# Four more query tiles turned by way of DRAM and VectorE in an adaLN block with linear attention

## The chip, the core and the metric

The kernel runs on one core of a Trainium2 chip. The metric is the device time of one execution in microseconds (us). Before the change three runs took 558.2, 560.55 and 560.79 us, a median of 560.55 us. A profile was taken of one more execution.

## What is computed

A block of x (2048 tokens of width 512, float32) with two halves. Each half normalises its input, scales and shifts it by vectors that come from a condition c, and adds a gated result to x.

```python
mod = (_silu(c) @ w_mod).reshape(1, 6, 1, -1)
sa, ca, ga, sb, cb, gb = (mod[:, i] for i in range(6))
h = _layernorm(x) * (1 + ca) + sa
x = x + ga * attention(h, wqkv, wo)
h = _layernorm(x) * (1 + cb) + sb
x = x + gb * (((h @ w_gate) * (h @ w_up)) @ w_down)      # 512 -> 1376 -> 512
...
# attention: 32 heads of 16
pq, pk = phi(q), phi(k)          # phi(t) = (t + 1 if t > 0 else exp(t)) + 1e-6
kv  = einsum("bhsd,bhse->bhde", pk, v)
z   = einsum("bhsd->bhd", pk)
num = einsum("bhqd,bhde->bhqe", pq, kv)
den = einsum("bhqd,bhd->bhq", pq, z)[..., None] + 1e-6
out = (num / den) @ wo
```

## The kernel before

**Tiles and stages.** The tokens lie in 16 tiles of 128 (numbered 0 to 15, so "tiles 5 to 8" counted from one are 4 to 7), four to a chunk. Every float32 product is made of three matmuls: both operands are split into a high part, made by ScalarE, and a low part, the difference, made by VectorE or GpSimd (`split`). The first stage makes k, sums up kv and z over all tiles and makes a part of q. The second makes W' = kv times wo with the gate ga in it (`w_out`), the denominators and, for each tile, y = x + (pq/den) W'. The third normalises y and runs the gated product over 1376 columns; three of its eleven column groups (`lone`) are computed early, while the attention of later chunks still runs, and the other eight in a block scheme with fewer products (`block`, `ffn`).

**The order of the work.** The program is written out by hand in the order in which each engine is to take its instructions; nothing is reordered. Each engine works through its own list and stops where an operand, or a buffer that is to be written, isn't ready. All transfers are issued by SP, one queue in that same order; a transfer whose source isn't there yet holds up those behind it. Eight semaphores go round among the transfers, so that each also waits for the one eight places before it. 94 buffers of 128 x 512 are handed out in turn, and so are eight banks of PSUM, four of them (`bank`) for passing results, four (`acc_bank`) for sums.

**One query tile, the first way (tiles 0 to 7).** `q_a` and `q_b` make phi(q). `den_a` multiplies it by z and sums over each head, `den_b` completes the denominators of a chunk and inverts them, `den_c` multiplies the tile by its inverse denominators. `turn_a` transposes the tile, which is 128 tokens by 512 columns, with four TensorE transposes into a bank (L672). `turn_h` (ScalarE) and `turn_l` (VectorE) split the result. `y_seed` copies x into a bank of sums (L746), and `y_a` adds twelve matmuls with W' (L755). `y_b` takes the sum back to SBUF with its statistics.

**The second way (tiles 8 to 15, `FLIPPED`).** `ready` is `den_c` and then `move_out`: the scaled tile is stored in DRAM. `move_in` fetches it back in four pieces, in which a 32-row block has become a column group. `turn_v` is one VectorE instruction that transposes 32 x 32 blocks (L722). Together they give the transposed tile with its columns in another order, and the matching W' has its rows in that order too (`wp4`): `wp_store` writes W' to DRAM, `wp_fetch` reads it back permuted. TensorE has no part in it.

**Around the change.** `y_step(i)` turns tile i + 1, makes y of tile i, splits and seeds tile i + 1 and takes back tile i - 1. `proj` makes q of a tile, `ln2_nx` normalises a chunk, `ln2_turn` transposes and modulates it, `gate_up` makes the two products of one of the `lone` groups and returns the rest (`g`), `split_gu`, `split_down` and `scale_down` prepare its weights. `by_fours` stores a column vector to DRAM, element by element, and fetches it back in groups of four for use much later (`flipped`). At the start of the third stage `right_sums` and `right_split` prepare the weights of the block scheme and `first[k].split` two of its left operands; `block` starts with its product of bank a, a second one in bank d, and a third one that adds to a copy of bank a.

Of the kernel before, what the change touches and what calls it, by code (L numbers as in the profile page):

```python
# [14 lines left out]
P = 128  # L15
# [9 lines left out]
def tile_adaln_block(  # L25
# [12 lines left out]
    nc = tc.nc  # L38
# [3 lines left out]
    KD = D // P  # L42
# [261 lines left out]
    def proj(i, w, of=bank):  # L304

        ch, j = divmod(i, NJ)
        ps = of()
        product(ps, [(cut(norm[ch].t[k], j * P, (j + 1) * P), w[k]) for k in range(KD)])
        return ps
# [48 lines left out]
    def q_b(i):  # L358
        phi_b(q_ps.pop(i), phq[i])
# [226 lines left out]
    def den_a(ch, *js, on=None):  # L586

        for j in js:
            den_p(ch, j, on=on)
            den_r(ch, j)  # L590
# [5 lines left out]
    def den_c(*tiles):  # L596

        for i in tiles:
            ch, j = divmod(i, NJ)
            p3 = phq[i].rearrange("p (h i) -> p h i", i=DH)  # L600
            nc.vector.scalar_tensor_tensor(p3, p3, EPS_PHI, dens[ch][:, j].unsqueeze(2).to_broadcast([P, NH, DH]),
                                           op0=ALU.add, op1=ALU.mult)
# [81 lines left out]
        turn_h(i)  # L684
        turn_l(i)

    FLIPPED = range(8, NT)
    SUMS = (0, 1, 2)
    wp4, moved = [], {}

# [49 lines left out]
    def y_seed(i, of=acc_bank):  # L740

        yps[i] = of()
        if of is bank:

            nc.tensor.matmul(yps[i], wp[0][0][:, :P], wp[0][0], start=True, stop=True)
        nc.scalar.activation(yps[i], xts[i // NJ][i % NJ], AF.Copy)  # L746

    def y_a(i):
# [17 lines left out]
    def y_step(i, *more, late=(), q=None, turn=True, seed=acc_bank):  # L766

        if q is not None:
            ps = proj(q, wq)
        if turn and i + 1 < NT and i + 1 not in pqs and i + 1 not in FLIPPED:  # L770
            turn_a(i + 1)
        y_a(i)
        if i + 1 in tps:
            turn_h(i + 1)
            turn_l(i + 1)
        if seed is acc_bank and i + 1 < NT:
            y_seed(i + 1, seed)
        if i - 1 in yps:
            y_b(i - 1)
        if q is not None:  # L780
            q_a(q, ps)
        if seed and i + 1 < NT and i + 1 not in yps:
            y_seed(i + 1, seed)
        for do in more:
            do()
        for do in late:
            do()
# [14 lines left out]
    def scale_down(f):  # L802
        d = raw_f[f][2]
        nc.vector.tensor_tensor(d, d, gb[:d.shape[0]], op=ALU.mult)  # L804

    def split_gu(f, low=None):
        n = fts[f][1]
        wf[f] = [split_raw(raw, (P, KD, n), low) for raw in raw_f[f][:2]]
# [62 lines left out]
    def ln2_nx(ch):  # L871
        norm2[ch].nmr_of()
        ln2_xhat(ch)

    def by_fours(col, name):

        t, v = consts.tile([P, KD], F32, name=name), tc.dram_tile([D], F32, name=name + "_row")
        nc.sync.dma_start(v.rearrange("(k p) -> p k", p=P), col)
        nc.sync.dma_start(t, v.rearrange("(p k) -> p k", k=KD))
        return t  # L880

    def stow(ch, *js):

# [29 lines left out]
    for f in lone:  # L913
        load_ffn(f)
    kept = [[tc.dram_tile([P, D], F32, name=f"kept_{ch}_{k}") for k in range(KD)] for ch in PLAIN]
    cb4, sb4 = by_fours(cb, "cb4"), by_fours(sb, "sb4")
    for ch in range(NCH):
        norm2[ch] = Norm(xts[ch])

# [290 lines left out]
    den_c(2)  # L1210
    q_a(11, ps)
    q_b(10)
    y_step(0, lambda: den_c(3), lambda: q_b(11))
    y_step(1)
    y_step(2, lambda: split_gu(f0, nc.gpsimd))
    y_step(3, lambda: scale_down(f0), wp_store, turn=False, seed=False)
    ps12 = proj(12, wq)
    y_b(3)
    norm2[0].rstd_of()
    den_a(1, 0, on=nc.vector)  # L1220
    q_a(12, ps12)
    ps13 = proj(13, wq)
    ln2_nx(0)
    q_b(12)
    den_a(1, 1, 2, on=nc.vector)
    q_a(13, ps13)
    ps14 = proj(14, wq, acc_bank)
    split_down(f0, nc.gpsimd)
    den_a(1, 3, on=nc.vector)
    den_b(1)  # L1230
    ln2_turn(0, 0, 1, cast=nc.vector)
    q_b(13)
    ps15 = proj(15, wq, acc_bank)
    ln2_turn(0, 2, 3, cast=nc.vector)
    q_a(14, ps14)
    den_c(4)
    q_b(14)
    q_a(15, ps15)
    split_gu(f1, nc.gpsimd)
    g = gate_up(0, f0)  # L1240
    q_b(15)
    den_c(5)
    scale_down(f1)
    g()
    turn(4)
    y_seed(4)
    split_gu(f2)
    g = gate_up(0, f1)
    den_a(2, 0, on=nc.vector)
    den_c(6)  # L1250
    split_down(f1, nc.gpsimd)
    g()
    y_step(4, lambda: scale_down(f2), lambda: den_a(2, 1, on=nc.vector))
    g = gate_up(0, f2)
    split_down(f2)
    den_c(7)
    den_a(2, 2, on=nc.vector)
    g()
    y_step(5, lambda: den_a(2, 3, on=nc.vector), wp_fetch)
    y_step(6, lambda: den_b(2), lambda: ready(8))  # L1260
    y_step(7, lambda: ready(9), lambda: move_in(8), turn=False, seed=False)
    y_b(7)
# [8 lines left out]
    ln2_turn(1, 2, 3)  # L1271
    y_step(9, lambda: turn_v(11))
    side.update(plain_side((0, 1)))
    first = [Left((0, 1), k).into(side) for k in range(KH)]
    for x in first:
        x.get("a21", "a22", "a11", "a12")
# [40 lines left out]
    first[1].sum("s1", "s3", "s2", "s4", on=nc.gpsimd)  # L1317
    y_seed(14, y_bank)
    turn_h(14)
    first[0].split("s1", "s2")  # L1320
    turn_l(14)
    y_b(13)
    y_seed(15, y_bank)
    right_sums(0, nc.vector)
    take()
    first[1].split("s1", "s2")
    turn_v(15)
    for n in range(4):
        banks.append(bank())
    banks[:] = [banks[n] for n in (2, 0, 1, 3)]  # L1330
    turn_bank[0] = acc_bank
    right_split(0)
    draw_load(0)
    stash, second_side, plan = {}, {}, {}
    work = ffn()
# [79 lines left out]
```

## Time and profile before

| | |
|---|---|
| runs | 558.2, 560.55, 560.79 us |
| profiled execution | 559.39 us |
| its span, first to last instruction | 557.7 us |
| granted TensorE clock, mean | 0.997 |
| TensorE matmul | 99% of the span |
| VectorE | 68% |
| ScalarE | 52% |
| GpSimd | 36% |

The page lists busy time by engine (PE is TensorE, DVE is VectorE, ACT is ScalarE, POOL is GpSimd, SPq the queue that issues transfers), groups of equal instructions, and a chain of waits: the work that ended last, followed back from the end, with start, length and name of each piece. The timeline has start, length, engine, line, operation, result and operands of each instruction; in square brackets stands how long the engine had been idle before it and what ended that. VectorE and ScalarE instructions overlap a little, so that the distance of two starts is less than the duration shown.

### The profile page before, as it was taken

How to read it: one execution, taken by the hardware profiler on the slowest of the kernel's cores; microseconds unless marked ns; L12 is line 12 of the kernel's file. 1: busy time of each engine (PE TensorE's matmuls, PEld its weight loads, DVE VectorE, ACT ScalarE, POOL GpSimd, SP SyncE). 2: the span in 40 equal slices, each digit the busy share in tenths (PEclk: the TensorE clock that was granted, in tenths of full speed). 3: DMA queues.
4: the chain of work that ended last, by engine and by line, in shares of the span. 5: the costliest groups of instructions: out<-in, count | busy, mean ns of one | idle time of the engine just before them, and what ended most of it. 6: DMA issues, size and time to landing. Idle time of an engine off the chain costs nothing.

```text
span 557.7 us, 7356 instructions
## 1 busy us (share of the span) xinstructions
PE 550.1 (99%) x2505; PEld 451.3 (81%) x2505; DVE 377.8 (68%) x605; ACT 291.4 (52%) x539; POOL 203.0 (36%) x203
## 2 busy tenths in 40 slices
PE   8999999999999999999899999999999999999997
PEld 6888888888888878878688888887888888888886
DVE  7896968977947886877877587886553544434435
ACT  3695856646477567566683545554444444444110
POOL 2000000101012300055698666566667446446200
PEclk9899999999999999999999999999999999999999
DMA  8900203220532605846435162591335222100004
GB/s 279 384 16 2 75 25 103 101 76 1 155 100 92 188 20 169 264 143 162 132 75 148 42 201 65 188 318 29 113 114 150 59 56 58 56 21 0 1 0 150
DMA packets 59141, 60.39 MB, mean 108 GB/s; under 512 B 8608, under 2 KB 37536, under 8 KB 59104
## 3 DMA queue, kind: packets, MB, share of 16 engines
q1 hardware_dynamic: 59104, 59.93, 34.3%
q8 instruction: 19, 0.31, 0.2%
q14 instruction: 18, 0.15, 0.1%
HBM read 43.65 MB, written 16.26 MB: 107 GB/s over the span
## 4 chain that ended last, share of the span: by engine, by line
PE 92%; DVE 3%; ACT 2%; DMA 1%; issue 1%; SPq 0%; DVEq 0%; ACTq 0%
PE bank L1026 32%; PE acc L1106 6%; PE acc L1107 6%; PE acc L1108 6%; PE acc L755 5%; PE bank L209 5%; PE bank L211 5%; PE bank L210 5%; PE acc L351 3%; PE acc L349 3%; PE acc L350 3%; PE bank L839 2%; PE bank L837 2%; PE bank L838 2%; PE bank L272 2%; DMA x<-in_A_x_dram 1%
## 5 line engine op out<-in xcount | busy, mean ns | idle before, releaser
L1026 PE MATMUL bank<-h,w 128*128 128x512 f32 (+1 forms) x798 | 185.4, 390 | 1.5 <-ACT bank L1031 1.5
L1026 PEld LDWEIGHTS bank<-h,w 128*128 128x128 f32 (+1 forms) x798 | 148.1, 186 | 35.8 <-ACT bank L1031 2.6
L1031 ACT ACTIVATE bank<-bank 128x512 f32<-128x512 f32 (+1 forms) x38 | 22.1, 583 | 137.1 <-PE bank L1026 137.0
L824 DVE TENSOR_TENSOR x<-acc,x 128x512 f32<-128x512 f32 (+1 forms) x73 | 48.4, 681 | 47.4 <-PE acc L1108 47.3
L1012 POOL TENSOR_TENSOR w<-raw,w 128x256 fp32r<-128x256 f32 (+3 forms) x38 | 41.3, 1086 | 95.2 <-ACT w L1005 95.2
L1107 PE MATMUL acc<-w,kh 128*128 128x512 f32 (+2 forms) x154 | 59.6, 387 | 0.0
L1106 PE MATMUL acc<-w,kh 128*128 128x512 f32 (+2 forms) x154 | 59.6, 387 | 0.0
L1108 PE MATMUL acc<-w,kl 128*128 128x512 f32 (+2 forms) x154 | 59.5, 386 | 0.0
L197 POOL TENSOR_TENSOR w<-raw,w 128x512 fp32r<-128x512 f32 (+1 forms) x25 | 36.0, 1442 | 55.3 <-ACT w L196 28.5
L250 POOL TENSOR_TENSOR rstd<-ve,half 128x4 f32<-128x4 f32 (+1 forms) x10 | 10.8, 1080 | 120.7 <-DVE ve L249 68.0
L1012 POOL TENSOR_TENSOR w<-t,w 128x512 fp32r<-128x512 f32 (+1 forms) x38 | 49.3, 1320 | 0.0
L197 DVE TENSOR_TENSOR kl<-u,kh 128x512 fp32r<-128x512 f32 (+1 forms) x38 | 26.4, 733 | 30.2 <-ACT kh L196 30.2
L209 PE MATMUL bank<-w,h 128*128 128x512 f32 x104 | 40.8, 392 | 0.0
L211 PE MATMUL bank<-w,h 128*128 128x512 f32 x104 | 40.5, 390 | 0.0
L210 PE MATMUL bank<-w,h 128*128 128x512 f32 x104 | 40.5, 389 | 0.0
L755 PE MATMUL acc<-w,xh 128*128 128x512 f32 x120 | 37.7, 395 | 0.0
L1106 PEld LDWEIGHTS acc<-w,kh 128*128 128x128 f32 (+1 forms) x154 | 28.9, 188 | 6.0
L1108 PEld LDWEIGHTS acc<-w,kl 128*128 128x128 f32 (+1 forms) x154 | 28.9, 188 | 5.9
L1107 PEld LDWEIGHTS acc<-w,kh 128*128 128x128 f32 (+1 forms) x154 | 28.9, 188 | 5.9
L1085 DVE TENSOR_TENSOR u<-bank,u 128x512 f32<-128x512 f32 (+1 forms) x19 | 13.1, 687 | 28.9 <-PE bank L1026 22.9
L259 ACT ACTIVATE n<-x,nmr,rstd 128x512 f32<-128x512 f32 x30 | 22.9, 804 | 12.2 <-DVE nmr L254 12.2
L196 ACT ACTIVATE w<-raw 128x512 fp32r<-128x512 f32 (+2 forms) x44 | 26.3, 619 | 1.9 <-DVE raw L804 1.0
(206 smaller groups left out, 1125.1 us busy)
## 6 DMA issues: line engine op xcount, KB each, us to landing
raw<-in_w_mod_dram SPq DMA_DIRECT2D x24, 256.0 KB, 3.8
raw<-in_B_w_down_dram SPq DMA_DIRECT2D x20, 256.0 KB, 3.2
raw<-in_B_w_gate_dram SPq DMA_DIRECT2D x36, 128.0 KB, 3.7
raw<-in_B_w_up_dram SPq DMA_DIRECT2D x36, 128.0 KB, 3.6
x<-in_A_x_dram SPq DMA_DIRECT2D x16, 256.0 KB, 5.7
out_dram<-x SPq DMA_DIRECT2D x15, 256.0 KB, 2.6
raw<-in_A_wqkv_dram SPq DMA_DIRECT2D x12, 256.0 KB, 5.4
wp<-w SPq DMA_DIRECT2D x8, 256.0 KB, 3.3
```

What stands on the lines that cost most here:

```text
L196: nc.scalar.activation(h, src, AF.Copy)
L197: (low or nc.vector).tensor_tensor(l, src, f32(h), op=ALU.subtract)
L209: nc.tensor.matmul(ps, ah, bh, start=i == 0, stop=False)
L210: nc.tensor.matmul(ps, ah, bl, start=False, stop=False)
L211: nc.tensor.matmul(ps, al, bh, start=False, stop=i == n - 1)
L755: nc.tensor.matmul(yps[i], x, y, start=False, stop=k == KD - 1 and x is al, skip_group_check=True)
L824: nc.vector.tensor_tensor(xt[:, a:b], dn[j][:, a:b], xt[:, a:b], op=ALU.add)
L1012: sub = lambda out, x, y: (on or nc.gpsimd).tensor_tensor(out, x, f32(y), op=ALU.subtract)
L1026: mm = lambda x, y, **kw: nc.tensor.matmul(ps, x[:, k], y, skip_group_check=True, **kw)
L1106: nc.tensor.matmul(ps, hh[:, a:b], dh[:n, c:d], start=i == 0, stop=False)
L1107: nc.tensor.matmul(ps, hh[:, a:b], dl[:n, c:d], start=False, stop=False)
L1108: nc.tensor.matmul(ps, hl[:, a:b], dh[:n, c:d], start=False, stop=i == len(hs) - 1)
```

## The change

Tiles 4 to 7 go the second way as well. For this `FLIPPED` starts at 4, `wp_store` stands behind `y_step(0)` and `wp_fetch` behind `y_step(2)`, the denominators of the second chunk are made between the steps of the first, and the calls of `ready`, `move_in`, `turn_v` and, for tile 4, `turn_h` and `turn_l` take the places of `den_c` and `turn`. `by_fours` is cut in two: the store stays, the fetch, which waits for it, is issued behind `y_step(9)`. `y_seed` no longer opens a passing bank with a matmul. At the start of the third stage the order of `turn_v(15)`, `turn_h(15)`, `right_sums`, the splits and `take` is another, and the four banks of the block scheme are no longer permuted.

```diff
-    FLIPPED = range(8, NT)
+    FLIPPED = range(4, NT)
...
     def y_seed(i, of=acc_bank):
 
         yps[i] = of()
-        if of is bank:
-
-            nc.tensor.matmul(yps[i], wp[0][0][:, :P], wp[0][0], start=True, stop=True)
         nc.scalar.activation(yps[i], xts[i // NJ][i % NJ], AF.Copy)
...
         nc.sync.dma_start(v.rearrange("(k p) -> p k", p=P), col)
-        nc.sync.dma_start(t, v.rearrange("(p k) -> p k", k=KD))
-        return t
+
+        def back():
+            nc.sync.dma_start(t, v.rearrange("(p k) -> p k", k=KD))
+            return t
+        return back
...
-    cb4, sb4 = by_fours(cb, "cb4"), by_fours(sb, "sb4")
+    back = by_fours(cb, "cb4"), by_fours(sb, "sb4")
...
-    y_step(0, lambda: den_c(3), lambda: q_b(11))
-    y_step(1)
-    y_step(2, lambda: split_gu(f0, nc.gpsimd))
-    y_step(3, lambda: scale_down(f0), wp_store, turn=False, seed=False)
+    y_step(0, lambda: den_c(3), lambda: q_b(11), wp_store)
+    y_step(1, lambda: den_a(1, 0, on=nc.vector))
+    y_step(2, lambda: split_gu(f0, nc.gpsimd), wp_fetch)
+    den_a(1, 1, on=nc.vector)
+    y_step(3, lambda: scale_down(f0), turn=False, seed=False)
+    den_a(1, 2, 3, on=nc.vector)
+    den_b(1)
     ps12 = proj(12, wq)
     y_b(3)
     norm2[0].rstd_of()
-    den_a(1, 0, on=nc.vector)
+    ready(4)
     q_a(12, ps12)
     ps13 = proj(13, wq)
+    ready(5)
     ln2_nx(0)
     q_b(12)
-    den_a(1, 1, 2, on=nc.vector)
+    ready(6)
+    move_in(4)
     q_a(13, ps13)
     ps14 = proj(14, wq, acc_bank)
     split_down(f0, nc.gpsimd)
-    den_a(1, 3, on=nc.vector)
-    den_b(1)
+    ready(7)
+    move_in(5)
     ln2_turn(0, 0, 1, cast=nc.vector)
     q_b(13)
     ps15 = proj(15, wq, acc_bank)
     ln2_turn(0, 2, 3, cast=nc.vector)
+    move_in(6, 7)
     q_a(14, ps14)
-    den_c(4)
+    turn_v(4)
     q_b(14)
     q_a(15, ps15)
     split_gu(f1, nc.gpsimd)
     g = gate_up(0, f0)
     q_b(15)
-    den_c(5)
+    turn_v(5)
     scale_down(f1)
     g()
-    turn(4)
+    turn_h(4)
+    turn_l(4)
     y_seed(4)
     split_gu(f2)
     g = gate_up(0, f1)
+    turn_v(6)
     den_a(2, 0, on=nc.vector)
-    den_c(6)
     split_down(f1, nc.gpsimd)
     g()
     y_step(4, lambda: scale_down(f2), lambda: den_a(2, 1, on=nc.vector))
     g = gate_up(0, f2)
+    turn_v(7)
     split_down(f2)
-    den_c(7)
     den_a(2, 2, on=nc.vector)
     g()
-    y_step(5, lambda: den_a(2, 3, on=nc.vector), wp_fetch)
+    y_step(5, lambda: den_a(2, 3, on=nc.vector))
...
     side.update(plain_side((0, 1)))
+    cb4, sb4 = (x() for x in back)
     first = [Left((0, 1), k).into(side) for k in range(KH)]
...
     turn_h(14)
-    first[0].split("s1", "s2")
+    turn_v(15)
+    right_sums(0, nc.vector)
     turn_l(14)
+    turn_h(15)
     y_b(13)
     y_seed(15, y_bank)
-    right_sums(0, nc.vector)
+    first[0].split("s1", "s2")
+    right_split(0)
+    first[1].split("s1", "s2")
     take()
-    first[1].split("s1", "s2")
-    turn_v(15)
+    turn_l(15)
     for n in range(4):
         banks.append(bank())
-    banks[:] = [banks[n] for n in (2, 0, 1, 3)]
     turn_bank[0] = acc_bank
-    right_split(0)
     draw_load(0)
```

## The prediction

> **What bounds the kernel now.** I read the page's first part, then TensorE's waits.
>
> ```profile
> span 557.7 us, 7356 instructions
> PE 550.1 (99%) x2505; PEld 451.3 (81%) x2505; DVE 377.8 (68%) x605; ACT 291.4 (52%) x539; POOL 203.0 (36%) x203
> ...
> PE bank L1026 <- ACT bank L1031: 1.5, 1, 1.5
> ```
>
> TensorE is busy 550.1 of 557.7 us. Past the start it waits once, at the first products of the last stage (1.5). So a gain can only be TensorE work that goes, or that 1.5; and every new wait of TensorE is lost whole. The chain of waits shows what the transposes cost, and what holds up the 1.5:
>
> ```profile
> 185.65 0.44 PE bank L672 x4
> ...
> 192.22 2.75 PE acc L755 x12
> ...
> 203.71 0.44 PE bank L672 x4
> 204.14 5.49 PE acc L755 x24
> ...
> 238.15 0.24 PE bank L839
> ...
> 263.79 2.29 DVE h L197 x2
> 266.08 1.02 DVE f L722
> ...
> 267.66 0.59 ACT bank L1031
> ```
>
> Four transposes take 0.44 us, and one matmul in a full stream 0.23 to 0.24. The last rows are the wait: VectorE turns tile 15 (`turn_v(15)`, L722) only at 266.08, behind two low parts that took 2.29. ScalarE's `turn_h(15)` waits for that, and the copy of bank a into bank b (L1031), on which TensorE's third product hangs, stands behind `turn_h(15)`.
>
> **The change part by part.** *Removed on TensorE*: 16 transposes (tiles 4 to 7; the first and the last four stand above), 4 x 0.44 = 1.76 us, and the matmul that opened tile 8's bank, 0.23. All lie in TensorE's unbroken stream: together 1.99.
>
> *The wait at 268*. `turn_v(15)` now stands right behind `turn_v(14)` (256.10, in the fence on VectorE's prices below) and takes 1.02 as at 266.08, so it ends near 258.2 and `turn_h(15)` soon after; the copy's place on ScalarE is then free. Gain 1.51, as that wait has it. What is late next: ScalarE now makes the four high parts of `right_split(0)` ahead of `first[1].split`.
>
> ```profile
> 263.89 0.62 ACT L1008 ACTIVATE w<-raw 128x512 fp32r<-128x512 f32 x1
> ...
> 263.59 3.19 PE L1026 MATMUL bank<-h,w 128*128 128x512 f32 x12
> 268.29 3.02 PE L1026 MATMUL bank<-h,w 128*128 128x512 f32 x12 [1.51 <-ACT bank L1031]
> ...
> 263.73 3.50 POOL L1012 TENSOR_TENSOR w<-t,w 128x512 fp32r<-128x512 f32 x2
> ```
>
> ScalarE is through with those at 264.4, so the first high part of `first[1]` is there at 265.0 and its low part, in the stretch where two of them took 2.29 beside GpSimd, at about 266.1. The second product wants it at its fifth matmul, 263.59 + 10 x 0.227 = 265.9. I charge 0.3: nothing if the low part takes 0.69 alone, 1.4 if it waits out GpSimd's pair (to 267.2).
>
> *Added on VectorE*: four turns for tiles 4 to 7, in place of four scalings (`den_c`, L601) that go forward into 169 to 174.
>
> ```profile
> 183.22 0.68 DVE L601 SCALAR_TENSOR_TENSOR h<-h,den 128x512 f32<-128x512 f32 x1
> 183.82 1.28 DVE L317 SCALAR_TENSOR_TENSOR h<-acc,h 128x512 f32<-128x512 f32 x2
> 185.02 0.94 DVE L601 SCALAR_TENSOR_TENSOR h<-h,den 128x512 f32<-128x512 f32 x1
> 185.89 1.78 DVE L804 TENSOR_TENSOR raw<-raw,row 128x512 f32<-128x512 f32 x1
> ...
> 189.57 0.68 DVE L680 TENSOR_TENSOR xl<-bank,xh 128x512 fp32r<-128x512 f32 x1
> ...
> 192.65 1.06 DVE L601 SCALAR_TENSOR_TENSOR h<-h,den 128x512 f32<-128x512 f32 x1
> 193.64 0.68 DVE L846 TENSOR_TENSOR phi<-bank,phi 128x512 f32<-128x512 f32 x1
> ...
> 198.74 0.68 DVE L601 SCALAR_TENSOR_TENSOR h<-h,den 128x512 f32<-128x512 f32 x1
> 199.34 0.68 DVE L578 TENSOR_TENSOR f<-h,zb 128x512 f32<-128x512 f32 x1
> ...
> 200.66 0.68 DVE L846 TENSOR_TENSOR phi<-bank,phi 96x512 f32<-96x512 f32 x1
> ...
> 256.10 1.10 DVE L722 STREAM_TRANSPOSE f<-u 128x512 f32<-128x512 f32 x1
> ```
>
> By the starts the scalings took 0.60, 0.87, 0.99 and 0.60 = 3.06; four turns of 1.02 take 4.08. VectorE so has 1.02 more here, less a head start: the second half of `ln2_turn(0)` hangs on ScalarE (179.76, below), and with no denominators queued VectorE is done with it at 182.6 instead of 183.22. It reaches the product of `gate_up(0, f2)` (L846, 200.66) 1.02 - 0.6 = 0.4 late, while TensorE comes 1.76 early. Who waits for it: that product releases ScalarE's split, then `turn_h(6)`, then tile 6's seed, one behind the other.
>
> ```profile
> 179.76 1.45 ACT L284 ACTIVATE f<-bank,col,col 128x512 f32<-128x512 f32 x2 [2.17 <-PE bank L272]
> ...
> 201.37 0.63 ACT L196 ACTIVATE kh<-phi 96x512 fp32r<-96x512 f32 x1 [0.93 <-DVE phi L846]
> ...
> 202.39 0.59 ACT L746 ACTIVATE acc<-x 128x512 f32<-128x512 f32 x1
> ```
>
> The seed (L746) ends at 202.98, and 203.4 after the change. `y_a(6)` stands in the chain at 204.14, where each matmul is entered at the end of the one before, about 0.23 after its own start; less that and less 1.76 it would start at 202.15. TensorE waits 203.4 - 202.15 = 1.25; I charge 1.3. Bounds: 0 if VectorE is not late (the seed then goes with TensorE), 1.25 + 0.6 + 0.27 + 0.39 = 2.5 if the head start of 0.6 goes and two turns are stretched as the scalings at 185.02 and 192.65 were. Tile 4 has room: its low part (189.57) came at 190.25, and `y_a(4)`, 192.22 in the chain, goes 0.88 forward, to 191.3.
>
> [...]
>
> *Moved forward on VectorE*: four `den_a` of 1.32 each (L578 and its sum, 199.34 to 200.66) and `den_b`.
>
> ```profile
> 169.07 0.17 DVE L247 TENSOR_SCALAR ve<-sums 128x4 f32<-128x4 f32 x1 [5.02 <-ACT acc L238]
> ...
> 171.43 2.92 ACT L259 ACTIVATE n<-x,nmr,rstd 128x512 f32<-128x512 f32 x4
> ...
> 175.67 0.87 PE bank L272 x8
> ```
>
> VectorE idled 5.02 ahead of `rstd_of` (L247), and some more between the tiles' low parts. Ten operations at 0.66 are 6.6, of which about 6 find a place there, so L247 comes some 0.5 late and the four normalisations (L259, done at 174.35) at most as much; TensorE transposes them at 175.67. The cover is 1.3, and I charge nothing; if GpSimd's splits drag the products out by 2, 1.2 would be lost.
>
> *Moved and added on SP's queue*: four stores and sixteen fetches of the tiles; the stores of wo' (`wp_store`) and the refetch (`wp_fetch`) early; the two fetches of `by_fours` late.
>
> ```profile
> 162.58 4.88 SPq L695 DMA_DIRECT2D wp<-w  x8
> 176.95 4.61 SPq L286 DMA_DIRECT2D kept<-f  x4
> ...
> w<-wp SPq DMA_DIRECT2D x8, 256.0 KB, 5.9
> moved<-h SPq DMA_DIRECT2D x8, 256.0 KB, 2.1
> u<-moved SPq DMA_DIRECT2D x32, 64.0 KB, 2.0
> cb_row<-col SPq DMA_DIRECT2D x1, 2.0 KB, 8.8
> ...
> 145.03 0.42 SPq L878 DMA_DIRECT2D cb_row<-col  x1
> ```
>
> Before, the stores of wo' began at 162.58, behind the two fetches that wait for scattered stores of 8.8 us. Now they go out as wo' is split, the last two after the scatters, 145.03 + 8.8 = 153.8 and a little; eight issues of 0.61 and a landing of 5.9 bring the refetch in before 170, against a first use (`y_a(4)`) near 191. Tile 4 is scaled at 170, stored by 172.4, issued back behind tile 6's store by 174.7 (0.43 each) and landed at 176.7; VectorE takes it at 182.6: 5.9 of cover. Tiles 6 and 7 stand behind the four stores of `kept` (to 181.6), land at 185.6 and 187.7, and are taken at 191.3 and 198. I charge nothing. The late `by_fours` fetches put 0.7 ahead of loads that are used many microseconds later: nothing, and 0.7 if that were wrong.
>
> *Sum*: -1.76 - 0.23 - 1.51 + 1.3 + 0.3 = -1.9. The profiled execution took 559.39 us, 557.7 of it the span; that gives 557.5. It lies 1.16 under the median of 560.55 (runs 558.2 to 560.79), so the forecast is 0.34% under its own execution and 0.54% under the median.
>
> **The rivals.** *VectorE keeps up.* TensorE gains all: 559.39 - 3.5 = 555.9. For it: 1.1 of the 1.78 at 185.89 is waiting beside GpSimd, and may shrink. Against: the products at 193.64 and 200.66 come without idle time of VectorE before them, so added work there shows.
>
> *VectorE sets the pace in both stretches.* If the head start goes and the charges reach their upper ends (2.5 + 1.4), the gain is undone: 559.39 - 3.5 + 3.9 = 559.8. For it: the stretch below, where VectorE (the third pair) is busy 9.86 of 10. Against: the 5 us of idle ahead of 169 take up most of what is moved.
>
> ```profile
> 178.00:188.00 10.00, 10.00 (x51) 8.02 (x50) 9.86 (x16) 5.34 (x9) 3.00 (x2) 1.00 0.74 222
> ```
>
> [...]
>
> *The turn waits for its transfer (slower).* `turn_v(4)` stands at VectorE's head at 182.6; behind it are `q_b(14)`, `q_b(15)`, the product of `gate_up(0, f0)` and all later low parts, and TensorE waits for those. From a landing at 183.7 (tile 4's low part has 191.3 - 190.25 = 1.05 of room) each microsecond is TensorE's. If store and fetch each took the 8.8 of the scatter, tile 4 would land at 170 + 8.8 + 1.8 + 8.8 = 189.4, 6.8 late, and tile 6's seed as much later than charged; with the 1.3 + 0.3 that is 559.39 - 3.5 + 6.8 + 1.6 = 564.3. Against: the landings of this very kind are 2.1 and 2.0.
>
> **How the numbers follow.** What this kernel's measurement can tell from no change is about 0.5%, 2.8 us. Chances: forecast 0.55, VectorE keeping up 0.20, pace 0.10, transfer 0.15. Against the median of 560.55 the line for faster is 557.75; the forecast lies just below it, and of its 0.55 I give 0.32 to faster and 0.23 to the same. With 0.19 of 0.20 from the first rival, faster is 0.51; the same is 0.23 + 0.01 + 0.10 = 0.34; slower 0.15. The predicted time is 557.5. The range goes from 555.4 (all 3.5 gained, and a run 0.5 lower) to 560.4 (nothing gained, and a run 0.5 higher), which leaves the transfer's case out.
>
> **What would show it.** The wait of TensorE on L1031 at 268 is gone, and `turn_v(15)` ends before 260. The chain has a stretch of VectorE and ScalarE ahead of `y_a(6)`, with TensorE idle 1.3 there. The second product of the last stage waits a few tenths on a low part (L197). No turn of tiles 4 to 7 waits for a transfer. It would be wrong if TensorE waited on `turn_v(4)`'s chain before 192, if the transposes at 175.67 came late, or if the stall at 268 were still there under another name.

## The result, and the profile after

Seven runs of the changed kernel took 561.56 to 565.03 us, a median of 563.06; beside them the kernel before took 558.55 (seven runs, 558.2 to 560.79). The ratio is 1.0069 with a 95% interval of 1.0044 to 1.0095: the change makes the kernel 0.7% slower. The profiled execution took 563.06 us, 561.4 of it the span, where the one of before had 557.7. The page and TensorE's waits:

```profile
span 561.4 us, 7362 instructions
PE 551.5 (98%) x2488; PEld 450.9 (80%) x2488; DVE 384.3 (68%) x609; ACT 291.6 (52%) x539; POOL 202.4 (36%) x203
...
PEclk9999999999999999999799999999999999999999
...
PE bank L1026 <- DVE h L197: 3.4, 2, 2.4
PE acc L148 <- DVE w L143: 2.0, 1, 2.0
PE acc L752 <- ACT acc L743: 0.9, 1, 0.9
```

17 matmul records fewer, and still 1.4 us more busy time. The wait on L1031 is gone; in its place stand 0.9 ahead of tile 6 and two waits, 3.4 together, at L1026 on VectorE's low parts (L197). The clock row has a 7 in one slice, in the same place. Four points of TensorE's timeline, in each kernel the first y matmul of the second stage, the first of tile 14, the first of tile 15, and one group of the block scheme behind it. Before:

```profile
155.41 0.70 PE L755 MATMUL acc<-w,xh 128*128 128x512 f32 x2
...
260.86 0.39 PE L755 MATMUL acc<-w,xh 128*128 128x512 f32 x1
...
271.15 0.61 PE L755 MATMUL acc<-w,xh 128*128 128x512 f32 x2
...
302.53 0.84 PE L1026 MATMUL bank<-h,w 128*128 128x512 f32 x3
```

After:

```profile
154.83 0.70 PE L752 MATMUL acc<-w,xh 128*128 128x512 f32 x2
...
259.42 0.62 PE L752 MATMUL acc<-w,xh 128*128 128x512 f32 x2
...
268.28 0.62 PE L752 MATMUL acc<-w,xh 128*128 128x512 f32 x2
...
306.25 0.62 PE L1026 MATMUL bank<-h,w 128*128 128x512 f32 x2
```

Two stretches by engine, before and then after; the column behind POOL is the granted clock:

```profile
10.00:20.00 10.00, 9.77 (x51) 8.01 (x52) 8.70 (x18) 8.31 (x14) 0.00 (x0) 0.83 1.05 391
274.50:281.20 6.70, 6.70 (x31) 5.53 (x31) 4.86 (x8) 2.50 (x6) 6.59 (x6) 1.00 0.25 65
```

```profile
10.00:20.00 10.00, 10.00 (x61) 8.38 (x60) 8.53 (x18) 8.11 (x14) 0.00 (x0) 1.00 1.05 390
274.50:281.20 6.70, 5.45 (x13) 4.30 (x14) 4.55 (x7) 1.11 (x2) 1.92 (x2) 0.50 0.17 42
```

The first pair of points differs by 0.58, which is no work of the change: from 10 to 20 us this execution of before had a clock of 0.83, that of after 1.00. (Of the fourteen kernels profiled for this text, the four whose clock falls early have the first point at 155.24 to 155.51, with the tiles or without, and the ten others at 154.21 to 154.94. Three of the four have 0.83 there, before, the new opening alone and the later rounding; the fourth, the rounding put back with the denominators behind, has an 8 in the clock row's slice from 14 to 28 us.) From the first point to the second the change gains 0.86 (105.45 to 104.59), to the third 1.43 more (10.29 to 8.86: the wait at 268 is gone), and to the fourth it loses 6.59 (31.38 to 37.97). Together -0.58 - 0.86 - 1.43 + 6.59 = +3.72, the difference of the spans. So one stretch of some ten microseconds takes back the gain three times over.

Here is that stretch, first before (VectorE's four low parts of s3 and s4, ScalarE's first rounding of the second k side, and GpSimd's low parts of it):

```profile
271.19 2.49 DVE L197 TENSOR_TENSOR h<-s,h 128x512 fp32r<-128x512 f32 x4
...
272.68 0.42 ACT L1005 ACTIVATE w<-raw 128x256 fp32r<-128x256 f32 x1
...
273.18 1.70 POOL L1012 TENSOR_TENSOR w<-raw,w 128x256 fp32r<-128x256 f32 x1 [4.73 <-ACT w L1005]
274.85 2.54 POOL L1012 TENSOR_TENSOR w<-t,w 128x512 fp32r<-128x512 f32 x2
277.34 1.29 POOL L1012 TENSOR_TENSOR w<-raw,w 128x512 fp32r<-128x512 f32 x1
```

and after, with TensorE's two waits:

```profile
270.56 5.73 DVE L197 TENSOR_TENSOR h<-s,h 128x512 fp32r<-128x512 f32 x4
...
268.97 0.41 ACT L1005 ACTIVATE w<-raw 128x256 fp32r<-128x256 f32 x1
...
269.45 0.90 POOL L1012 TENSOR_TENSOR w<-raw,w 128x256 fp32r<-128x256 f32 x1 [2.27 <-DMA u<-stowed]
270.32 3.15 POOL L1012 TENSOR_TENSOR w<-t,w 128x512 fp32r<-128x512 f32 x2
273.44 1.70 POOL L1012 TENSOR_TENSOR w<-raw,w 128x512 fp32r<-128x512 f32 x1
...
272.39 0.97 PE L1026 MATMUL bank<-h,w 128*128 128x512 f32 x3 [0.99 <-DVE h L197]
275.75 8.57 PE L1026 MATMUL bank<-h,w 128*128 128x512 f32 x25 [2.39 <-DVE h L197]
```

ScalarE came to L1005 3.7 us sooner (272.68 to 268.97) and VectorE to its low parts only 0.6 (271.19 to 270.56). Before, VectorE was 2.0 ahead of GpSimd and done when the latter had hardly begun; now GpSimd is 1.1 ahead, and the four low parts take 5.73 in place of 2.49. It isn't that both run slower for some reason: alone VectorE needs 2.49 and GpSimd 2.54 + 1.29 for the last three, 6.32 in sum, and together they took 270.32 to 276.29, 5.97. They ran nearly one after the other. The products s3 x t3 wait for it: from the matmul at 271.01 to 275.75 TensorE does four in 4.74, where four take 0.91, a loss of 3.83. Its clock is at 0.50 from 274.5 to 281.2 (the last row of the windows above), so that from 275.75 on it loses half of 5.45, 2.73. 3.83 + 2.73 = 6.56 of the 6.59.

This collision is the first theory for the experiments (Theory A below); that the waits bring the clock down is its second half.

### The profile page after: what moved, and what is told of

The parts are those of the page before. It is cut to its first block, busy times and chain, and to the rows that moved or that the text cites. A ratio compares the mean times of both kernels' runs of the same rounds, so it can differ in the third digit from the quotient of the medians.

```text
span 561.4 us, 7362 instructions
## 1 busy us (share of the span) xinstructions
PE 551.5 (98%) x2488; PEld 450.9 (80%) x2488; DVE 384.3 (68%) x609; ACT 291.6 (52%) x539; POOL 202.4 (36%) x203
## 4 chain that ended last, share of the span: by engine, by line
PE 88%; DVE 6%; ACT 3%; issue 1%; DMA 1%; SPq 0%; DVEq 0%; ACTq 0%
PE bank L1026 32%; PE acc L1107 6%; PE acc L1106 6%; PE acc L1108 6%; PE bank L209 5%; PE bank L210 5%; PE bank L211 5%; PE acc L752 4%; PE acc L351 3%; PE acc L350 3%; PE acc L349 3%; PE acc L148 2%; PE bank L272 2%; DVE h L197 1%; DVE f L722 1%
## 5 line engine op out<-in xcount | busy, mean ns | idle before, releaser
L1026 PE MATMUL bank<-h,w 128*128 128x512 f32 (+1 forms) x798 | 188.6, 394 | 3.4 <-DVE h L197 3.4
L1026 PEld LDWEIGHTS bank<-h,w 128*128 128x128 f32 (+1 forms) x798 | 149.8, 189 | 39.3 <-DVE h L197 4.7
L1031 ACT ACTIVATE bank<-bank 128x512 f32<-128x512 f32 (+1 forms) x38 | 22.1, 583 | 138.8 <-PE bank L1026 138.8
L821 DVE TENSOR_TENSOR x<-acc,x 128x512 f32<-128x512 f32 (+1 forms) x73 | 48.4, 680 | 47.4 <-PE acc L1108 47.4
L1012 POOL TENSOR_TENSOR w<-raw,w 128x256 fp32r<-128x256 f32 (+3 forms) x38 | 41.6, 1095 | 93.7 <-ACT w L1005 91.4
L197 POOL TENSOR_TENSOR w<-raw,w 128x512 fp32r<-128x512 f32 (+1 forms) x25 | 34.9, 1401 | 56.3 <-ACT w L196 56.3
L1012 POOL TENSOR_TENSOR w<-t,w 128x512 fp32r<-128x512 f32 (+1 forms) x38 | 49.4, 1319 | 0.0
L197 DVE TENSOR_TENSOR kl<-u,kh 128x512 fp32r<-128x512 f32 (+1 forms) x38 | 26.8, 745 | 31.6 <-ACT kh L196 31.6
L1085 DVE TENSOR_TENSOR u<-bank,u 128x512 f32<-128x512 f32 (+1 forms) x19 | 13.1, 689 | 27.9 <-PE bank L1026 21.7
```

The lines of the kernel that those rows point to most:

```text
L197: (low or nc.vector).tensor_tensor(l, src, f32(h), op=ALU.subtract)
L821: nc.vector.tensor_tensor(xt[:, a:b], dn[j][:, a:b], xt[:, a:b], op=ALU.add)
L1012: sub = lambda out, x, y: (on or nc.gpsimd).tensor_tensor(out, x, f32(y), op=ALU.subtract)
L1026: mm = lambda x, y, **kw: nc.tensor.matmul(ps, x[:, k], y, skip_group_check=True, **kw)
```

## The experiments

Each run was timed in turns with the kernel before on the same chip; its median was 558.64 to 558.82 there.

**Which part of the change.** The opening of the last stage undone in the changed kernel, and done alone in the kernel before (the last hunk of the change, backward and forward).

```diff
     turn_h(14)
-    turn_v(15)
-    right_sums(0, nc.vector)
+    first[0].split("s1", "s2")
     turn_l(14)
-    turn_h(15)
     y_b(13)
     y_seed(15, y_bank)
-    first[0].split("s1", "s2")
-    right_split(0)
-    first[1].split("s1", "s2")
+    right_sums(0, nc.vector)
     take()
-    turn_l(15)
+    first[1].split("s1", "s2")
+    turn_v(15)
...
+    right_split(0)
     draw_load(0)
```

The permutation of the banks goes with it. This is the first run's edit to the changed kernel; the second makes the reverse edit to the kernel before.

> The changed kernel with one part undone: the order of the last stage's opening (from the seed of the last y step to the first load of the draw) is that of before; the regrouped tiles 5 to 8, the earlier denominators and the moved loads stay. Theory A (the opening's new order makes the loss: ScalarE is free 3.7 us earlier, so GpSimd's low parts of the k side fall on VectorE's low parts of s, TensorE waits 3.4 us and its granted clock falls to 0.5 for some 6 us): the low parts on VectorE take 0.6 us each again, the three waits on them (0.99, 2.39) are gone, the granted clock at 274 to 282 is 1.00, the 1.5 us wait at 268 is back, and the time is about 1.4 us below before (ratio about 0.9975, some 557 us). Theory B (it is the arrival 1.4 us earlier, made by the tiles, that brings the collision): the waits and the clock of 0.5 stay, ratio 1.005 or more.

> The kernel before with one part of the change alone: the new order of the last stage's opening; tiles 5 to 8 are turned by TensorE as before. Theory A: the collision of the low parts comes without the tiles as well; VectorE's low parts of s take about 1.4 us each, TensorE waits some 3.4 us in the 6 us behind the last y step, its granted clock is near 0.5 for some 6 us, and the time is 3.5 to 5 us above before (ratio 1.006 to 1.009). Theory B: the low parts take 0.6 us, the 1.5 us wait is gone, and the time is 0 to 1.5 us below before (ratio 0.997 to 1.000).

Measured: 558.09 (ratio 0.9985, 0.9973 to 0.9997) with the old opening, 563.12 (1.0073, 1.0057 to 1.0089) with the new one alone. First the low parts and GpSimd's first one with the old opening, then those of the new opening alone:

```profile
267.02 3.03 PE L1026 MATMUL bank<-h,w 128*128 128x512 f32 x12 [1.49 <-ACT bank L1031]
...
269.92 2.49 DVE L197 TENSOR_TENSOR h<-s,h 128x512 fp32r<-128x512 f32 x4
...
271.91 1.70 POOL L1012 TENSOR_TENSOR w<-raw,w 128x256 fp32r<-128x256 f32 x1 [4.73 <-ACT w L1005]
```

```profile
270.86 0.92 POOL L1012 TENSOR_TENSOR w<-raw,w 128x256 fp32r<-128x256 f32 x1 [2.27 <-ACT w L1005]
...
271.98 5.72 DVE L197 TENSOR_TENSOR h<-s,h 128x512 fp32r<-128x512 f32 x4
...
277.16 7.13 PE L1026 MATMUL bank<-h,w 128*128 128x512 f32 x23 [2.39 <-DVE h L197]
```

Both as Theory A has it: the whole loss is the opening's, with the tiles or without them, and Theory B falls. The new opening alone can be laid beside the kernel before, as both traces have the first point at 155.4: ScalarE comes to L1005 at 270.38 in place of 272.68, and VectorE to its four low parts at 271.98 in place of 271.19. Of the 3.1 us by which VectorE's head start turns round (2.0 ahead to 1.1 behind), ScalarE and GpSimd coming sooner make 2.3, and VectorE coming later 0.8. The tiles, the denominators and the queue together gain (0.15%, 0.84 us of 558.77; Theory A's 1.4 is just inside the interval).

**The collision or the order.** Two kernels that part VectorE's and GpSimd's work in time: one by moving VectorE's sums, without which GpSimd's later low parts can't start, one by moving ScalarE's roundings alone.

```diff
-    right_sums(1, nc.vector)
     first[0].split("s3", "s4")
     fill(1)
     first[1].split("s3", "s4")
+    right_sums(1, nc.vector)
```

```diff
-    "p7": [lambda: draw_load(m + 1), lambda: right_load(m + 2), lambda: right_split(m + 1)],
-    "p3": [lambda: ds.append(split_raw(draw, low=nc.gpsimd))],
+    "p7": [lambda: draw_load(m + 1), lambda: right_load(m + 2)] + ([later] if m else []),
+    "p3": [lambda: ds.append(split_raw(draw, low=nc.gpsimd))] + ([] if m else [later]),
```

`later` is the call of `right_split(m + 1)`.

> The changed kernel with one step moved: VectorE makes the low parts of s3 and s4 of the last stage first and the sums of the k side behind them, so that GpSimd's low parts of t, which need these sums, start later. Theory A: the low parts of s take about 0.6 us each, TensorE's waits on them are below 0.5 us in all, the granted clock stays at 1.00 there, and the time is 5 to 6.5 us below the changed kernel: 556.5 to 558 us, ratio to before 0.994 to 0.999. A rival (GpSimd's first two low parts of the k side, which don't need the sums, collide all the same): the first of the low parts of s still take over 1 us, a wait of 1 to 2 us stays, and the ratio is 1.000 to 1.005; whether the clock falls then tells how long a wait it takes.

> The changed kernel with one step moved on ScalarE alone: its rounding of the second part of the k side stands behind its part of the draw's split, so that it and GpSimd's low parts behind it come later; the order on VectorE is that of the changed kernel, the sums still stand ahead of the low parts of s. If the two engines' work at one time is what makes the low parts slow (Theory A), these take 0.6 to 0.7 us each (2.5 us for the four; 5.73 in the changed kernel), TensorE's waits in the 6 us behind the last y step are 1 us or less in all, the granted clock stays at 1.00 there, and the time is 4 to 6 us below the changed kernel (ratio to before 0.995 to 0.999). If instead the sums ahead of them on VectorE make them late (the order, not the collision), TensorE still waits 2 us or more there, and the ratio is 1.003 or more.

Measured: 557.21 (0.9969, 0.9956 to 0.9981) with the sums behind, 558.25 (0.9991, 0.9982 to 1.0000) with the later rounding. In the second one VectorE's order is that of the changed kernel to the instruction:

```profile
270.44 2.49 DVE L197 TENSOR_TENSOR h<-s,h 128x512 fp32r<-128x512 f32 x4
...
275.54 1.18 POOL L1012 TENSOR_TENSOR w<-raw,w 128x256 fp32r<-128x256 f32 x1
...
276.77 11.46 PE L1026 MATMUL bank<-h,w 128*128 128x512 f32 x49 [0.45 <-POOL w L1012]
```

The low parts are back at 2.49 there, with VectorE's order unchanged and only ScalarE's roundings, and GpSimd's work behind them, later: it is the collision. This kernel is 4.8 us below the changed one, but gains less on before than the one with the sums behind; the k side is late now (0.45 on L1012). With the sums behind, the four take 3.01, a wait of 0.42 on VectorE (L1085) is left, and the kernel beats both; the rival of a wait of 1 to 2 us falls.

**The wait or the clock.** The changed kernel with matmuls that nobody reads in the gap, 16 and then 5. They had 512 columns each; the 64 in the first expectation is an error of that text. They write into a bank whose sums `take` has read by then. The edit with 16:

```diff
-    take = down(1, (2, 3))
+    spent = {j: acc_bank() for j in (2, 3)}
+    take = down(1, (2, 3), dn=spent)
...
     y_step(15)
+    for _ in range(16):
+        nc.tensor.matmul(spent[2], ones_r, wp4[0][0], start=True, stop=True)
```

> The changed kernel with 16 more products of 64 columns, whose results nobody reads, behind the last y step, where TensorE waits for the low parts of s. It separates the wait from the clock. If the waits bring the clock down (Theory A), the granted clock at 274 to 282 stays at or near 1.00 though the low parts come as late as in the changed kernel, and the time is 1.5 to 3 us below the changed kernel (560 to 561.5 us). If the clock falls for another reason (the load of this stretch, the chip), it is 0.5 to 0.6 there again, and the time is that of the changed kernel or up to 1 us more.

> The changed kernel with 5 products of 512 columns that nobody reads behind the last y step, in place of the 16 of the run kept busy (which had 512 columns each too, 0.23 us). They cover the first of the two waits (0.99 us), while the second (2.39 us) stays about 2.2 to 2.4 us long. It asks how much waiting it takes for the clock to fall. If one wait of over 2 us is enough: granted clock 0.5 to 0.7 for 4 to 8 us behind it, and the time of the changed kernel (some 563 us, ratio 1.006 to 1.008). If it takes the sum of the two within 5 us: the clock stays at 1.00 and the time is that of the run kept busy (ratio 1.002 to 1.004).

Measured: 560.72 (1.0032, 1.0022 to 1.0042) with 16, 560.68 (1.0037, 1.0023 to 1.0050) with 5. With 16, the added matmuls (L1356) fill the gap to within a tenth, and the window behind them has its full clock:

```profile
270.83 3.79 PE L1356 MATMUL acc<-w,ones_r 128*128 128x512 f32 x16
274.46 9.86 PE L1026 MATMUL bank<-h,w 128*128 128x512 f32 x41
```

```profile
274.50:281.20 6.70, 6.61 (x29) 5.10 (x28) 5.90 (x10) 1.76 (x4) 2.48 (x3) 1.00 0.25 66
```

VectorE is as late as in the changed kernel (5.79 for the four), and the clock stays up: the fall comes from the wait, and costs 563.06 - 560.72 = 2.3 us of the loss (2.1 by the two ratios), against 2.73 counted in the one profile. With 5, the profiled execution shows one wait and then a slow clock for 3.4 us:

```profile
275.17 13.03 PE L1026 MATMUL bank<-h,w 128*128 128x512 f32 x49 [2.40 <-DVE h L197]
```

```profile
276.40:279.80 3.40, 3.40 (x10) 2.66 (x9) 1.97 (x4) 1.11 (x2) 1.28 (x1) 0.54 0.00 0
```

That execution took 561.67. Of the five, this one and one of 561.49 have a mean clock of 0.996, the others (560.62 to 560.68, the time of the kernel kept busy) 0.999. So by the mean clocks this gap brought the clock down in two executions of five, and the expectation of an either-or fell. Only the first of the five has a trace, and one execution with 16 matmuls has 0.996 too (561.2), with its gap filled. How long a wait it takes is not settled beyond this.

**Which step of the opening.** I sharpened Theory A: the freed ScalarE alone is the price. One run does only the step that frees ScalarE, on top of the old opening; one takes only the early rounding of the first k side back out of the new opening.

```diff
     turn_h(14)
+    turn_v(15)
     first[0].split("s1", "s2")
...
     first[1].split("s1", "s2")
-    turn_v(15)
```

```diff
     first[0].split("s1", "s2")
-    right_split(0)
     first[1].split("s1", "s2")
...
     draw_load(0)
+    right_split(0)
```

> The run with the old opening (0.9985) with one step of the new one: VectorE's transpose of tile 15 stands behind the high part of tile 14 again, as in the changed kernel; the sums, the splits, the seeds and the banks keep the order of before. It is that step by which ScalarE's stall of 2.6 us ahead of the copy at L1031 goes. Theory A sharpened (the collision is the price of that very stall: whatever frees ScalarE brings GpSimd's low parts of the second k side onto VectorE's low parts of s): the 1.5 us wait of TensorE is gone, ScalarE's first rounding of the second k side starts near 269 to 270 in place of 272 to 273, the low parts of s take over 1.2 us each, TensorE waits 2 to 3.5 us for them, the clock falls, and the ratio is 1.004 to 1.008. Rival (it is the rest of the new order, the early sums and the early rounding of the first k side, that makes the collision): the low parts take 0.6 us, nothing but a wait under 0.5 us is left, and the ratio is 0.995 to 0.997.

> The changed kernel with one step of the opening put back: ScalarE rounds the first k side behind the first load of the draw, as before, and not ahead of the first part of s of the second pair. ScalarE's stall ahead of the copy at L1031 stays away, since the transpose of tile 15 keeps its early place. Theory A: ScalarE has the same work ahead of the second k side and no stall, so the collision stays (low parts over 1.2 us each, waits of 2 to 3.5 us, clock down, ratio 1.005 to 1.009). Rival (the early rounding of the first k side is what brings the second one forward): the low parts take 0.6 us, no wait over 0.5 us, ratio 0.995 to 0.998. A third outcome: the first products of the stage now wait for the first k side itself, over 1 us at 262, with or without the collision.

Measured: 558.13 (0.9987, 0.9978 to 0.9996) for the transpose alone, 557.42 (0.9972, 0.9961 to 0.9982) with the rounding put back. First the transpose alone, then the rounding put back:

```profile
268.59 4.13 DVE L197 TENSOR_TENSOR h<-s,h 128x512 fp32r<-128x512 f32 x4
...
269.52 0.96 POOL L1012 TENSOR_TENSOR w<-raw,w 128x256 fp32r<-128x256 f32 x1 [2.27 <-ACT w L1005]
...
275.08 13.22 PE L1026 MATMUL bank<-h,w 128*128 128x512 f32 x57 [1.12 <-DVE u L1085]
```

```profile
263.54 5.39 PE L1026 MATMUL bank<-h,w 128*128 128x512 f32 x22 [0.52 <-POOL w L1012]
...
269.02 2.49 DVE L197 TENSOR_TENSOR h<-s,h 128x512 fp32r<-128x512 f32 x4
...
270.30 2.41 POOL L1012 TENSOR_TENSOR w<-raw,w 128x256 fp32r<-128x256 f32 x1 [2.61 <-DMA u<-stowed]
```

The sharpened theory fell, and so did the rival of the first run. The rival of the second has its numbers (2.49 for the four, 0.9972, waits of 0.52 and less) but not its mechanism. With the transpose alone, ScalarE's L1005 starts at 269.04, as foretold, and GpSimd comes 2.4 us sooner than with the old opening (269.52 for 271.91), but VectorE is still 0.9 ahead: the low parts are half stretched, and the wait of 1.49 has become one of 1.12 and one of 0.34 (on L1012, at 267.31). With the rounding put back, ScalarE comes to the second k side at 269.78, only 0.8 later than in the changed kernel, yet VectorE is 1.5 sooner (269.02 for 270.56) and ahead by 1.3. What held VectorE back in the changed kernel are its low parts of s1 and s2. There, ScalarE's high parts for the second pair stand behind the rounding, and that pair then runs beside GpSimd's low parts of the first k side:

```profile
260.61 1.29 DVE L197 TENSOR_TENSOR h<-s,h 128x512 fp32r<-128x512 f32 x2 [1.00 <-ACT h L196]
263.53 2.50 DVE L197 TENSOR_TENSOR h<-s,h 128x512 fp32r<-128x512 f32 x2 [1.62 <-ACT h L196]
```

With the rounding put back all four follow one another:

```profile
260.40 2.50 DVE L197 TENSOR_TENSOR h<-s,h 128x512 fp32r<-128x512 f32 x4 [1.00 <-ACT h L196]
```

That is 1.62 of idling and 1.2 of stretching, of which VectorE loses a part again further on. At the second k side it is GpSimd that stands still (2.41 for a low part that took 0.90 in the changed kernel). The third outcome came in small: the first products wait 0.20 and 0.52 for the first k side.

That left a third theory, that the early rounding and the early transpose together are enough:

```diff
     take()
+    right_split(0)
     first[1].split("s1", "s2")
...
-    right_split(0)
     draw_load(0)
```

> The run with the old opening and the early transpose of tile 15 (0.9987), with one line moved in addition: ScalarE rounds the first k side ahead of the first parts of s of the second pair, as the changed kernel does. Theory C (two steps make the loss together: this line makes VectorE wait for ScalarE and then run the first low parts of s beside GpSimd's of the first k side, so that it comes to the second low parts some 1.5 us later, when GpSimd has already begun those of the second k side): the low parts of s of the last y step take over 1.3 us each, TensorE waits 2.5 us or more for them, the granted clock falls to 0.5 to 0.7 for several us, and the ratio is 1.003 to 1.009. Rival (the early sums or the early high part of tile 15, which this run doesn't have, are needed for it): the waits stay at 1.5 us or less, the clock at 1.00, ratio 0.997 to 1.000.

Measured: 558.65 (0.9993, 0.9979 to 1.0007). The four low parts take 4.13 again, from 268.90, GpSimd starts at 269.63, and TensorE waits 1.56 with its clock at 1.00. Theory C fell, and its rival holds but for a wait of 1.56 where it had at most 1.5: VectorE comes 1.7 sooner here than in the changed kernel. There the additions of `take()` (L821) stand behind the low parts of `first[1]`, which wait for ScalarE; here VectorE makes them in that wait. So the loss takes more of the new order than these two steps, and the further ones were not parted. Through all of these kernels it goes with VectorE's head start over GpSimd at the second k side:

| kernel | head start of VectorE, us | the four low parts, us | TensorE's wait for them or right behind, us | ratio |
|---|---|---|---|---|
| before | 2.0 | 2.49 | none | 1 |
| old opening, new tiles | 2.0 | 2.49 | none | 0.9985 |
| later rounding | 5.1 | 2.49 | 0.45, for the k side | 0.9991 |
| rounding put back | 1.3 | 2.49 | none | 0.9972 |
| sums behind | 0.9 | 3.01 | 0.42 | 0.9969 |
| transpose alone | 0.9 | 4.13 | 1.12 | 0.9987 |
| transpose and rounding | 0.7 | 4.13 | 1.56 | 0.9993 |
| new opening alone | -1.1 | 5.72 | 1.01 + 2.39 | 1.0073 |
| changed kernel | -1.1 | 5.73 | 0.99 + 2.39 | 1.0069 |

The head start isn't all: 0.9 costs 4.13 with the transpose alone and 3.01 with the sums behind, where GpSimd has only its first low part to make (269.17) and the next ones start at 272.83.

**What adds up.** Three runs: the new opening with the sums behind, but without the tiles; and, against the 0.9 us ahead of tile 6, the two good openings (sums behind, rounding put back) with one step more. The first joins edits shown above. The step more is

```diff
     split_down(f2)
-    den_a(2, 2, on=nc.vector)
     g()
-    y_step(5, lambda: den_a(2, 3, on=nc.vector))
+    y_step(5, lambda: den_a(2, 2, 3, on=nc.vector))
```

> The kernel before with the new order of the last stage's opening and the sums behind the low parts of s; tiles 5 to 8 are turned by TensorE as before. Theory A: the opening alone brings what it was to bring once the collision is out: the 1.5 us wait at 268 is gone, a wait of 0.4 us stays, the clock stays at 1.00, and the time is 0.8 to 1.3 us below before (ratio 0.9977 to 0.9986). With the run that has the old opening (0.9985) it adds up to the run that has both (0.9969). Rival: without the 1.4 us that the tiles bring, the order of arrival on ScalarE is another, and the collision or a wait over 2 us comes back: ratio 1.002 or more.

> The run with the sums behind the low parts of s (ratio 0.9969), with one step more: a part of the denominators of tiles 8 to 11 (1.4 us on VectorE) moves from ahead of the last phi of the third gate and up products to behind it, so that ScalarE's kh and the seed of tile 6 that stands behind it come up to 1.4 us sooner. Theory A (the 0.9 us wait on the seed ahead of y_a(6) hangs on that chain): the wait is under 0.2 us, the later stages move up by it, and the time is 0.7 to 0.9 us lower (ratio to before 0.995 to 0.996, some 556.4 us). Rival: the seed waits for TensorE's end of the products or the bank, then the wait stays 0.5 to 0.9 and the ratio 0.997; or the denominators come late for tiles 8 and 9, then a new wait on the queue's transfers is seen near 230 and the ratio is 0.998 or more.

> The run with the rounding of the first k side put back (0.9972), with the part of the denominators behind the last phi of the third gate and up products as well, the step that took the 0.9 us wait ahead of y_a(6) away. If the two add up, the wait ahead of y_a(6) is gone, only 0.5 to 0.8 us of waits at 262 to 264 are left of what the change brought, the clock is 1.00, and the ratio is 0.995 to 0.996 (556.0 to 556.5 us). Rival: coming 0.9 us earlier, the first products of the last stage wait that much longer for the first k side, which hangs on its own transfers; then the waits at 262 to 264 are 1.4 to 1.7 us and the ratio stays 0.997.

Measured: 558.22 (0.9986, 0.9974 to 0.9997) for the opening without the tiles; with the tiles' 0.9985 it makes 0.9971, and the run that has both 0.9969: they add up, as far as intervals of 0.0012 to each side can tell. The denominators behind gave 557.09 (0.9966, 0.9953 to 0.9979) with the sums behind, 557.17 (0.9970, 0.9958 to 0.9982) with the rounding put back. In both the wait on L743 is gone from the trace. The only wait of TensorE past the start that the first one's list has left:

```profile
PE bank L1026 <- DVE u L1085: 0.4, 1, 0.4
```

Its span is 0.8 shorter than without the step (554.5, 555.3). The second one's waits at 262 to 264 stay 0.19 and 0.52, so its rival of longer waits falls. Yet neither median goes below that of its base by more than the intervals allow (0.9966 against 0.9969, 0.9970 against 0.9972). The mean clock hides it: three of five and five of eight of their executions have 0.996 or 0.997, of the bases' ten each two and one, and in the one of these eight that has a trace the clock row is under 9 in one slice alone, from 14 to 28 us, far ahead of the step. Among the executions with 0.999 or 1.0 the step is seen: 556.17 and 556.23 against 556.82 to 557.42 with the sums behind, 556.14 to 556.62 (three) against 557.18 to 557.98 with the rounding put back. These are few, and were picked out afterwards. By their medians four kernels beat the one of before by 0.3%, and can't be told from one another.

## Why the prediction was wrong

The forecast of 557.5 us, faster, was wrong, and 563.06 lies outside its range. Against the seven runs of before (558.55) 557.5 is a gain of 0.2%, not the 0.54% that the first three runs' 560.55 made of it. The upper end, 560.4, is not what its own words give: 559.39 and 0.5 are 559.9. Step by step:

- *The transposes and the matmul of tile 8's bank, -1.99, and the seed of tile 6, +1.3.* Right in kind and in sum. Forecast -0.69, measured -0.86 at tile 14. The wait ahead of tile 6 has the place and the chain forecast; it is 0.89 in place of 1.25, as VectorE's product came 0.23 late (200.31 less the 200.66 - 0.58 of before) and not 0.4. That it came so near is partly luck. The head start of 0.6 isn't there (the first turn starts at 182.80, for 183.22 - 0.58 = 182.64 before), but the multiplication by a row that took 1.78 at 185.89 takes 0.69 now: GpSimd's pair beside it ended at 186.15, just as that one began. Taking the 0.89 off leaves a gain of 1.75, so some 0.2 of the 1.99 isn't found. The chain of waits after, ahead of tile 6:

```profile
199.71 0.04 DVE den L584
...
200.31 0.69 DVE phi L843
...
201.02 0.63 ACT kh L196
201.65 0.52 ACT xh L676
202.17 0.49 ACT acc L743
...
202.71 3.47 PE acc L752 x14
```

- *The denominators forward and the queue, nothing.* Right in the outcome: no turn of tiles 4 to 7 waited for a transfer, and TensorE waited for none of it. But the margin was nearly used up. L247 comes 1.6 late and not 0.5 (170.08 for 169.07 - 0.58), as two of the products moved forward ran beside a pair of GpSimd and took 1.79 and 1.06 for 0.68; the normalisations come 1.1 late, of a cover of 1.3.
- *The wait at 268, -1.51.* Right by itself: `turn_v(15)` is done before 257, and 1.43 is gained by tile 15.
- *What is late next: +0.3 on the low part of `first[1]`.* This is the step that failed. "The copy's place on ScalarE is then free" was taken as the end of the story, and the question of what comes next was asked for one operand, the low part that the second product takes. That wait isn't there at all. What the freed ScalarE does with the time wasn't asked: it comes 3.7 us sooner to the second k side and sets GpSimd going under VectorE's next four low parts, to which VectorE comes only 0.6 sooner, held up by the new order itself. In place of 0.3 this cost 3.83 of waiting and 2.73 of clock, 6.56 by the trace. The rows for it were in the profile of before: VectorE's four low parts from 271.19 on, and GpSimd idle 4.73 up to 273.18, held back by ScalarE. Which steps of the new order are needed for the loss, beyond those parted above, stays open.
- *The rivals.* None was this one. The slower rival's 564.3 is close to the time, but its mechanism, a late transfer, did not happen.

With one line put back, the rounding of the first k side, the same change runs at 557.42 (0.9972): 0.28% or 1.6 us below before, where the forecast's sum was 1.9. That the two are close is partly chance, as 0.72 of waits at 262 to 264 stand there for the 0.3, and 0.89 ahead of tile 6 for the 1.3.

The prediction reckoned with VectorE and GpSimd holding each other up at single rows: the two low parts that took 2.29 at 263.79, and the 1.78 at 185.89, beside which a pair of GpSimd ran from 184.12 to 187.12 (0.69 after). The traces show more of it where the loss is: 5.97 us for work that is 6.32 one after the other, and the loser is VectorE when it is 1.1 behind (5.73 for 2.49) and GpSimd when VectorE is 1.3 ahead (2.41 for 0.90, with the rounding put back). Why VectorE loses in part with a head start of 0.9, and with one of 1.3 where the denominators stand behind as well (3.04 for the four), isn't shown. The question should have been asked wherever the change moves either engine.

## What to carry to other kernels

When a change takes a stall away, follow the engine that it frees to its next instructions and the engines that these release, and lay their new times beside what runs there already; when VectorE and GpSimd come to overlapping work, look at their order: here 0.6 us in it (VectorE 1.3 ahead or 0.7) went with 1.56 us of waiting. Where one of two colliding operations feeds TensorE directly, let that one go first: here a head start of 1.3 us cost TensorE nothing, one of 0.7 to 0.9 up to 1.6, and a lag of 1.1 cost 3.8. A gap of TensorE such as the 2.4 us here has to be counted with the slow clock that may follow it, 2.73 us in the changed kernel.

## What the runs showed of the hardware

TensorE's clock fell to one half behind gaps of 2.39 and 2.40, and its cost is not in proportion to the gap. Waits of 1.51 (before), 1.49 and 1.56 left the clock at 1.00 in their profiles; one of 2.40 brought it down for 3.4 us; 0.99 and 2.39 with three matmuls between them brought it down from 274.5 to 281.2, 6.7 us, in the changed kernel, and 1.01 and 2.39 for about half as long, from 278.5 to 281.9, in the new opening alone. The longer is near twice the shorter. A gap is not the only cause: in four of the fourteen profiles, that of before among them, the clock falls early. In that of before it is at 0.50 for 3.4 us, from 15.7 to 19.1 (the 0.83 above), though TensorE had waited at most 0.40 at a time since 2.0; sixteen matmuls of one column run ahead of it (from 13.42 and 14.59), and what brings it down there was not tried. Why two executions of five have a mean clock of 0.996 and the others 0.999, with the five matmuls in the gap, isn't shown. The changed kernel's seven executions spread in the same way, from 561.56 (mean clock 0.997) to 565.03 (0.990), while eight of the nine with the gap filled lie at 560.46 to 560.90 with 1.0.
